# Scores, maxima and their riders in column tiles of 32 on TensorE, with 288 keys for 32 queries

## The chip, the cores and the metric

The kernel runs on one core of one Trainium2 chip. The metric is the device time of one execution in microseconds (us), lower is better. Three executions of the kernel before took 827.12, 827.70 and 828.55 us, median 827.7 us.

## What is computed

A transformer block on 2048 tokens of 512 features: a layer norm, then sliding-window attention and a gated feed-forward network beside each other, joined at the end.

```python
def _A_ref(x, wqkv, wo):            # H = 32 heads, Dh = 16, window W = 256
    scores = einsum("bhqd,bhkd->bhqk", q, k) * Dh ** -0.5
    mask = (idx[:, None] - idx[None, :] >= 0) & (idx[:, None] - idx[None, :] < W)
    p = softmax(where(mask, scores, -1e9)); o = einsum("bhqk,bhkd->bhqd", p, v)
    return o.transpose(...).reshape(B, S, D) @ wo
...
xn = layernorm(x); s = _A_ref(xn, wqkv, wo)
g = silu((silu(xn @ w1) * (xn @ w3)) @ w2)
return x + s * g
```

A query meets itself and the 255 keys before it. That is the fact which the change uses: 64 neighbouring queries together meet 64 + 255 keys, 32 neighbouring queries 32 + 255.

## The kernel before

The tokens are cut into four stretches t of 512, the heads into four groups g of eight, and each group into two pairs p of passes. That makes 32 **units** (t, g, p). Every fp32 product is made of fp16 terms (high and low halves), so a score contracts over 3 x 16 = 48 rows, and two heads lie in the two halves of the partitions (rows 0 and 64).

Attention goes in two passes for each unit.

- **Pass 1** (`pass1`, L605 to L643) finds each query's largest score. `part` makes one of eight score tiles, of 128 queries and two heads: query columns are stationary, and the keys stream past (L623). In all but the first 256 tokens it takes 64 queries at a time and streams the `WIN` = 320 keys that they may meet. With two heads that is four matmuls, each on one quarter of the array (48 rows by 64 columns). Where `narrow` is set, it takes 32 queries at a time, eight matmuls, still with 320 keys. Then VectorE adds the mask MW and takes the maximum along the keys, one instruction for each head (L637). After eight parts the maxima are scaled into NM (L642, L643).
- **`finish`** (L645 to L663) turns the maxima with two matmuls by the identity (L652) into spare columns of a score tile, and sends them by DMA into two more rows of qa, so that pass 2 subtracts them inside its matmul (50 rows).
- **Pass 2** (`pass2`, L678 on) makes the scores the other way round: 64 keys are stationary, and the queries that meet them stream (L699), in pieces of 64 to 320 columns. A chunk fills two banks of PSUM; VectorE masks its edges (L706), ScalarE takes the exponential (L709). `values` multiplies it with V in fp32 on tiles of 64 rows by 32 columns (L727).

**Riders** are small matmuls that use spare columns of a score tile of pass 1: the maxima's turn (L652), sums of squares for the scales of the weights (`powers`, L269 to L273), and the transposes of x for the next stretch (`turn_beside`, L480 to L488), eight fp32 matmuls a rider.

The dense work (the projections L567 and L537, gate and up L900, down L950, output L1001) uses the whole array with 512 moving columns. The order of the work on TensorE is written out by hand: `PLAN` gives each unit five batches of score work. A letter stands for one score tile: W is a chunk of pass 2; M, X and N are parts of pass 1, X into the bank of the value product and N narrow; the last batch, NN, is followed by the values. `spread` puts dense matmuls between batches. VectorE, ScalarE, GpSimd and the DMA queue get their order from a scheduler with priorities, and each of them works in order.

The masks are made once at the start: MW on 64 partitions by VectorE and GpSimd (L198 to L203), then copied to the other 64 with one DMA of SyncE's queue (L1179), between loads of weights (L804).

Of the kernel before, what the change touches and what calls it, by code (L numbers as in the profile page):

```python
# [11 lines left out]
BF16 = mybir.dt.bfloat16  # L12
F16 = mybir.dt.float16
# [8 lines left out]
P = 128  # L22
# [9 lines left out]
TW = S // NT  # L32
KW = TW + 2 * P
WIN = 64 + 2 * P
FB = F // P
NEG = -1e30

# [9 lines left out]
KR = TERMS * DH  # L47
# [32 lines left out]
def tile_block(ctx: ExitStack, tc: tile.TileContext, x, wqkv, wo, w1, w3, w2, out):  # L80
    nc = tc.nc
# [7 lines left out]
    const = pool("const", 1)  # L89
# [88 lines left out]
    def beside_scores(n, f):  # L178
# [4 lines left out]
    identf = const.tile([P, P], F32, name="identf")  # L183
# [11 lines left out]
    nc.gpsimd.affine_select(M1[:, 1, :], M1[:, 1, :], pattern=[[-1, P]], base=0, channel_multiplier=1,  # L195
                            compare_op=ALU.is_ge, fill=NEG)

    MW = const.tile([P, WIN], BF16, name="MW")  # L198
    nc.vector.memset(MW[0:64], 0.0)
    nc.gpsimd.affine_select(MW[0:64], MW[0:64], pattern=[[1, WIN]], base=0, channel_multiplier=-1,  # L200
                            compare_op=ALU.is_gt, fill=NEG)
    nc.gpsimd.affine_select(MW[0:64], MW[0:64], pattern=[[-1, WIN]], base=2 * P, channel_multiplier=1,
                            compare_op=ALU.is_ge, fill=NEG)  # L203


# [5 lines left out]
                                compare_op=ALU.is_gt if k else ALU.is_ge, fill=NEG)  # L211


    NM = [const.tile([P, 64], F16, name=f"NM{i}") for i in range(3)]
    for nm in NM:
        nc.gpsimd.memset(nm, 0.0)

# [40 lines left out]
    def powers(sb, n, p2, inv, s=None):  # L258


        m = sb.shape[-1] // n
        al = small.tile([P, n], F32, name="al")
        if s is None:
            ps = scores_bank()[:, 0, 0:n]
            for i in range(m):
                nc.tensor.matmul(ps, onesb, sb[:, i * n:(i + 1) * n], start=i == 0, stop=i == m - 1)
        else:
            for h in range(2):
                for c in range(2):  # L269
                    for i in range(m):  # L270
                        nc.tensor.matmul(s[64 * c:64 * c + 64, h, WIN:WIN + n],
                                         onesb[64 * h:64 * h + 64, 64 * c:64 * c + 64],
                                         sb[64 * h:64 * h + 64, i * n:(i + 1) * n], start=i == 0, stop=i == m - 1)  # L273

        def rest():
            if s is None:
                nc.vector.tensor_scalar(al, ps, 2.08, 1e-30, op0=ALU.mult, op1=ALU.max)
            else:
                with urgent():
                    nc.vector.tensor_scalar(al, s[:, 0, WIN:WIN + n], 2.08, 1e-30, op0=ALU.mult, op1=ALU.max)  # L280
                    nc.vector.scalar_tensor_tensor(al, s[:, 1, WIN:WIN + n], 2.08, al, op0=ALU.mult, op1=ALU.add)

            nc.vector.tensor_scalar(al.bitcast(I32), al.bitcast(I32), 24, 23, op0=ALU.logical_shift_right,  # L283
                                    op1=ALU.logical_shift_left)
# [114 lines left out]
    def prepare(t):  # L399
# [76 lines left out]
        def turn_beside(b, n, s):  # L476


            if t not in X:
                X[t] = xpool.tile([P, NC, TW], F16, name="XH"), xpool.tile([P, NC, TW], F16, name="XL")  # L480
            xh, xl = X[t]
            for k in range(n, n + 2):
                for h in range(2):
                    for c in range(2):
                        f = k * P + 64 * c
                        rows = slice(64 * h, 64 * h + 64)
                        nc.tensor.matmul(s[64 * c:64 * c + 64, h, WIN + 64 * (k - n):WIN + 64 * (k - n + 1)],
                                         xts[b][rows, f:f + 64], identf[rows, rows], start=True, stop=True)  # L488
            if n:
                give(xts.pop(b))  # L490

            def rest():
                pt = s[:, :, WIN:WIN + P].rearrange("p h (k q) -> p k h q", k=2)
                hi, lo = (a[:, n:n + 2, b * P:(b + 1) * P].rearrange("p k (h q) -> p k h q", h=2) for a in (xh, xl))
                with urgent():
                    nc.vector.tensor_copy(hi, pt)
                    nc.vector.tensor_sub(lo, pt, hi)
                if n:
                    turned[t] = turned.get(t, 0) + 1
            return rest  # L500
# [104 lines left out]
    def pass1(t, g, p):  # L605


        M = small.tile([P, 2, 2, 4], F32, name="M")
        whole = NM[(2 * (t * NG + g) + p) % len(NM)]
        nm = whole[:, 0:32].rearrange("p (b i) -> p b i", b=2)  # L610

        def part(ii, a, beside, narrow):
            qa, ka = QA[t, g], keys(t, g)
            i = t * 4 + ii
            n, mask = ((i + 1) * P, M1.rearrange("p a b -> p (a b)")[:, (1 - i) * P:]) if i < 2 else (WIN, MW)
            s = pso.tile([P, 2, TW], F32, name="po") if beside else scores_bank()

            w = 32 if narrow else 64
            for c in range(0, P, w):
                e = (ii + 3) * P if i < 2 else (ii + 2) * P + 64 * (c // 64 + 1)  # L620
                for r in range(2):
                    rows = slice(64 * r, 64 * r + KR)
                    nc.tensor.matmul(s[c:c + w, r, :n], qa[rows, 2 * p + a, ii * P + c:ii * P + c + w],  # L623
                                     ka[rows, 2 * p + a, e - n:e], start=True, stop=True)
            after = []
            if narrow:
                pass
            elif alone[0] and maxima and (ii, a) != (0, 0):
                after = [f(s) for f in maxima]
                maxima.clear()  # L630
            elif alone[0] and besides:
                after = [besides.pop(0)(s)]
            alone[0] = not after or t * NG + g <= 2
            for r in range(2):
                junk = ppool.tile([P, D], BF16, name="junk", bufs=1)
                with urgent():
                    lasts["maximum"] = nc.vector.tensor_tensor_reduce(  # L637
                        out=junk[:, :n], in0=s[:, r, :n], in1=mask, scale=1.0,
                        scalar=NEG, op0=ALU.add, op1=ALU.max, accum_out=M[:, r, a, ii:ii + 1])
            if (ii, a) == (3, 1):  # L640
                Mf = M.rearrange("p r a i -> p (r a i)")
                nc.vector.tensor_scalar(nm[:, 0, :], Mf, -1.0 / ONE, None, op0=ALU.mult)  # L642
                nc.vector.scalar_tensor_tensor(nm[:, 1, :], Mf, -1.0 / ONE, nm[:, 0, :], op0=ALU.mult, op1=ALU.subtract)  # L643
                maxima.append(finish)
            for f in after:  # L645
                f()

        def finish(s):

            for h in range(2):  # L650
                rows = slice(64 * h, 64 * h + 64)
                nc.tensor.matmul(s[0:64, h, 448:512], whole[rows, 0:64], identh[rows, rows], start=True, stop=True)  # L652

            def rest():
                qa = QA[t, g]
                mt = small.tile([32, P], F16, name="mt")
                with urgent():
                    nc.vector.tensor_copy(mt.rearrange("p (h q) -> p h q", h=2), s[0:32, :, 448:512])
                dm = dpool.tile([32, P], F16, name="dm")
                nc.sync.dma_start(dm, mt)  # L660
                for r in range(2):
                    nc.sync.dma_start(qa[64 * r + KR:64 * r + KR + 2, 2 * p:2 * p + 2, :].rearrange("p a q -> p (a q)"),
                                      dm.rearrange("(b r i) q -> r b (i q)", b=2, r=2)[r])  # L663
            return rest
        return [lambda *kind, ii=ii, a=a: part(ii, a, *kind) for ii in range(4) for a in range(2)]
# [12 lines left out]
    def pass2(t, g, p):  # L678
# [14 lines left out]
        def scores(c):  # L693
            qa, ka = QA[t, g], keys(t, g)
            s = scores_bank()
            for o, h, a, (m, k, n, _, _) in pieces(c):
                for r in range(2):
                    rows = slice(64 * r, 64 * r + KR + 2)
                    nc.tensor.matmul(s[64 * h:64 * h + 64, r, o:o + 64 * n], ka[rows, 2 * p + a, 64 * (m + 4):64 * (m + 5)],  # L699
                                     qa[rows, 2 * p + a, 64 * (m + k):64 * (m + k + n)], start=True, stop=True)  # L700
            which, *_, masks = chunks[c]
            sv = s.rearrange("p r (a k q) -> p (r a) k q", a=len(which), q=64)
            for first, by, n, kind, of in masks:
# [472 lines left out]
    qk[0][0]()  # L1176
    qk[1][0]()
    wv[0]()
    nc.sync.dma_start(MW[64:P], MW[0:64])  # L1179
    for i, k in enumerate((0, 2, 1)):  # L1180
        nc.sync.dma_start(MK[64:P, i], MK[0:64, k])
    load(0, 0)
# [152 lines left out]
```

## Time and profile before

| | |
|---|---|
| time, median of 3 | 827.7 us (827.12 to 828.55) |
| span of the profiled execution | 824.7 us |
| between the span and the median | 3.0 us |
| TensorE matmul busy | 803.9 us, 97% |
| TensorE weight loads | 380.7 us (beside the matmuls) |
| VectorE | 632.2 us, 77% |
| ScalarE | 388.8 us, 47% |
| GpSimd | 205.6 us, 25% |

The profiled execution's own time is known as its span, from the first to the last instruction; the 3.0 us around it lie outside the trace. In the rows that follow, PE is TensorE's matmuls, PEld its weight loads, DVE is VectorE, ACT ScalarE, POOL GpSimd and SPq the DMA queue of SyncE. A row of the timeline gives start and duration in us, engine, line, operation, tile written and tiles read, and their shapes; "48\*64 48x320" is a matmul with 48 rows by 64 columns of weights and 320 moving columns. Matmuls overlap: the duration of one is its whole way through the array, so the pace is read from starts, not from durations.

### The profile page before, as it was taken

How to read it: one execution, taken by the hardware profiler on the slowest of the kernel's cores; microseconds unless marked ns; L12 is line 12 of the kernel's file. 1: busy time of each engine (PE TensorE's matmuls, PEld its weight loads, DVE VectorE, ACT ScalarE, POOL GpSimd, SP SyncE). 2: the span in 40 equal slices, each digit the busy share in tenths (PEclk: the TensorE clock that was granted, in tenths of full speed). 3: DMA queues.
4: the chain of work that ended last, by engine and by line, in shares of the span. 5: the costliest groups of instructions: out<-in, count | busy, mean ns of one | idle time of the engine just before them, and what ended most of it. 6: DMA issues, size and time to landing. Idle time of an engine off the chain costs nothing. (4 is left out here: it accounts for less than half of the span.)

```text
span 824.7 us, 22891 instructions
## 1 busy us (share of the span) xinstructions
PE 803.9 (97%) x8924; PEld 380.7 (46%) x8924; DVE 632.2 (77%) x2021; ACT 388.8 (47%) x562; POOL 205.6 (25%) x355
## 2 busy tenths in 40 slices
PE   8999989999999999999999999999999999999998
PEld 4434435444445444444444444444444444444444
DVE  8788878887798678879878887778777787676435
ACT  6889775634435434344343444442433344343511
POOL 2238174332223203121211111230201113030201
PEclk9999989999999999999999999999999999999999
DMA  9978566266543354544433344434434353343101
GB/s 283 267 230 237 194 177 191 73 170 186 160 122 84 98 154 124 161 117 135 134 105 100 108 109 138 132 119 113 142 85 144 91 131 102 101 132 91 56 21 53
DMA packets 95325, 110.66 MB, mean 134 GB/s; under 512 B 17200, under 2 KB 60528, under 8 KB 95216
## 3 DMA queue, kind: packets, MB, share of 16 engines
q1 hardware_dynamic: 94928, 108.67, 45.9%
q8 instruction: 70, 1.15, 0.6%
q10 hardware_dynamic: 288, 0.52, 0.2%
q14 instruction: 39, 0.32, 0.1%
HBM read 76.28 MB, written 28.57 MB: 127 GB/s over the span
## 5 line engine op out<-in xcount | busy, mean ns | idle before, releaser
L311 POOL TENSOR_TENSOR slot<-slot,slot 128x256 f16<-128x256 f32 (+1 forms) x228 | 151.1, 690 | 522.3 <-ACT slot L929 406.9
L900 PE MATMUL m<-XH,slot 128*128 128x512 f16 x896 | 269.0, 382 | 6.3 <-DVE slot L924 3.2
L709 ACT ACTIVATE pt<-s,es 128x1024 f32<-128x1024 f32 x152 | 167.7, 1113 | 198.3 <-DVE s L706 196.4
L900 PEld LDWEIGHTS <-slot 128*128 128x128 f16 x1344 | 125.4, 98 | 162.6 <-issue 18.9
L900 PE MATMUL m<-XL,slot 128*128 128x512 f16 x448 | 170.5, 381 | 0.0
L950 PE MATMUL m<-slot,slot 128*128 128x512 f16 x672 | 156.5, 380 | 1.5 <-DVE slot L580 0.7
L706 DVE TENSOR_TENSOR s<-s,MK 128x256 f32<-128x256 f32 (+2 forms) x280 | 118.3, 435 | 49.4 <-PE s L699 47.0
L637 DVE CUSTOM_DVE_ANT_0 junk<-s,MW 128x320 bf16<-128x320 f32 x276 | 134.1, 486 | 24.6 <-PE s L623 15.8
L950 PEld LDWEIGHTS <-slot 128*128 128x128 f16 x672 | 61.9, 98 | 79.7 <-issue 9.0
L637 DVE CUSTOM_DVE_ANT_0 junk<-po,MW 128x320 bf16<-128x320 f32 x172 | 83.6, 486 | 5.4 <-DVE al L283 0.5
L727 PE MATMUL po<-pt,V 64*32 64x320 f32 (+4 forms) x2880 | 77.2, 342 | 0.1
L929 ACT CAST slot<-slot 128x512 f16<-128x512 f32 x56 | 34.5, 616 | 76.0 <-DVE slot L924 71.8
L915 ACT ACTIVATE slot<-m,sgs 128x512 f32<-128x512 f32 x56 | 38.3, 684 | 54.9 <-PE m L900 54.8
L727 PEld LDWEIGHTS po<-pt,V 64*32 64x32 f32 x2880 | 51.1, 106 | 21.6 <-issue 0.8
L919 DVE SCALAR_TENSOR_TENSOR slot<-slot,m 128x512 f32<-128x512 f32 x56 | 38.3, 684 | 27.6 <-ACT slot L915 27.3
L699 PE MATMUL s<-qa,KA 50*64 50x320 f16 (+3 forms) x1472 | 58.3, 260 | 0.6 <-ACT pt L709 0.6
L699 PEld LDWEIGHTS <-KA 50*64 50x64 f16 x1472 | 30.3, 106 | 55.3 <-issue 32.7
L623 PE MATMUL s<-KA,qa 48*64 48x320 f16 (+3 forms) x824 | 45.5, 295 | 4.3 <-ACT pt L709 3.2
L924 DVE SCALAR_TENSOR_TENSOR slot<-m,slot 128x512 f32<-128x512 f32 x56 | 38.5, 687 | 10.6 <-PE m L900 10.0
L974 DVE SCALAR_TENSOR_TENSOR slot<-m,dsc,slot 128x512 f32<-128x512 f32 x48 | 35.9, 747 | 13.2 <-PE m L950 13.0
L567 PE MATMUL m<-XH,whi 128*128 128x512 f16 x120 | 44.7, 381 | 0.0
L567 PE MATMUL m<-XL,whi 128*128 128x512 f16 x120 | 44.5, 379 | 0.0
(162 smaller groups left out, 870.6 us busy)
## 6 DMA issues: line engine op xcount, KB each, us to landing
slot<-dW SPq DMA_DIRECT2D x126, 256.0 KB
slot<-in_B_w_dram SPq DMA_DIRECT2D x42, 256.0 KB
dW<-slot SPq DMA_DIRECT2D x42, 256.0 KB
slot<-in_A_x_dram SPq DMA_DIRECT2D x30, 256.0 KB
KA<-dK SPq DMA_DIRECT2D x24, 288.0 KB
qa<-dQ SPq DMA_DIRECT2D x32, 192.0 KB
dQ<-slot SPq DMA_DIRECT2D x16, 256.0 KB
dK<-slot SPq DMA_DIRECT2D x16, 256.0 KB
```

Source lines behind the costliest of these rows:

```text
L311: op(out[:, c], a[:, c], b[:, c])
L567: nc.tensor.matmul(cell["pp"], a[:, k, c, :], b[:, c, :], start=(c, i) == parts[0][0], stop=(c, i) == parts[-1][-1])
L623: nc.tensor.matmul(s[c:c + w, r, :n], qa[rows, 2 * p + a, ii * P + c:ii * P + c + w], ka[rows, 2 * p + a, e - n:e], start=True, stop=True)
L637: lasts["maximum"] = nc.vector.tensor_tensor_reduce(out=junk[:, :n], in0=s[:, r, :n], in1=mask, scale=1.0, scalar=NEG, op0=ALU.add, op1=AL ...
L699: nc.tensor.matmul(s[64 * h:64 * h + 64, r, o:o + 64 * n], ka[rows, 2 * p + a, 64 * (m + 4):64 * (m + 5)], qa[rows, 2 * p + a, 64 * (m + k ...
L706: nc.vector.tensor_add(v, v, MK[:, kind, of:of + n, :].unsqueeze(1).to_broadcast([P, 2 * len(which), n, 64]))
L709: nc.scalar.activation(pt, s, AF.Exp, scale=es)
L727: nc.tensor.matmul(cell["po"][32 * i:32 * i + 32, h, 64 * (m + k):64 * (m + k + n)], V[64 * h:64 * h + 64, (4 * t + m // 2) % VB, hd * VW: ...
L900: nc.tensor.matmul(cell[k], w[:, (a * NC + c) * P:(a * NC + c + 1) * P], b[:, c, :], start=c == 0 and i == 0, stop=c == NC - 1 and i == 2)
L915: nc.scalar.activation(sg, cell[0], AF.Tanh, scale=sg_scale[:, f:f + 1])
L924: lasts["emptied"] = nc.vector.scalar_tensor_tensor(sg, cell[1], 0.5 * HS / (WS * XS)**2, sg, op0=ALU.mult, op1=ALU.mult)
L950: nc.tensor.matmul(ps, hh[:, a * TW + b * P:a * TW + (b + 1) * P], w[:, c * D:(c + 1) * D], start=f == f0 and i == 0, stop=f == f1 - 1 and ...
```

## The change

All matmuls of the score tiles take 32 columns of the array. Pass 1 always takes 32 queries at a time, with 288 keys (`MWIN`) in place of 320, and its mask and VectorE's instruction shrink with it. In pass 2 each stationary set of 64 keys becomes two of 32, with the same moving columns. The riders are split in the same way. MW is made on 32 partitions and copied with three DMAs in place of one. NM shrinks from 64 columns to 32.

```diff
+MWIN = 32 + 2 * P
...
-    MW = const.tile([P, WIN], BF16, name="MW")
-    nc.vector.memset(MW[0:64], 0.0)
+    MW = const.tile([P, MWIN], BF16, name="MW")
+    nc.vector.memset(MW[0:32], 0.0)
...
-    NM = [const.tile([P, 64], F16, name=f"NM{i}") for i in range(3)]
+    NM = [const.tile([P, 32], F16, name=f"NM{i}") for i in range(3)]
...
-                for c in range(2):
+                for c in range(0, P, 32):
                     for i in range(m):
-                        nc.tensor.matmul(s[64 * c:64 * c + 64, h, WIN:WIN + n],
-                                         onesb[64 * h:64 * h + 64, 64 * c:64 * c + 64],
+                        nc.tensor.matmul(s[c:c + 32, h, WIN:WIN + n], onesb[64 * h:64 * h + 64, c:c + 32],
                                          sb[64 * h:64 * h + 64, i * n:(i + 1) * n], start=i == 0, stop=i == m - 1)
...
-                    for c in range(2):
-                        f = k * P + 64 * c
+                    for c in range(0, P, 32):
+                        f = k * P + c
                         rows = slice(64 * h, 64 * h + 64)
-                        nc.tensor.matmul(s[64 * c:64 * c + 64, h, WIN + 64 * (k - n):WIN + 64 * (k - n + 1)],
-                                         xts[b][rows, f:f + 64], identf[rows, rows], start=True, stop=True)
+                        nc.tensor.matmul(s[c:c + 32, h, WIN + 64 * (k - n):WIN + 64 * (k - n + 1)],
+                                         xts[b][rows, f:f + 32], identf[rows, rows], start=True, stop=True)
...
-            n, mask = ((i + 1) * P, M1.rearrange("p a b -> p (a b)")[:, (1 - i) * P:]) if i < 2 else (WIN, MW)
+            n, mask = ((i + 1) * P, M1.rearrange("p a b -> p (a b)")[:, (1 - i) * P:]) if i < 2 else (MWIN, MW)
...
-            w = 32 if narrow else 64
+            w = 32
             for c in range(0, P, w):
-                e = (ii + 3) * P if i < 2 else (ii + 2) * P + 64 * (c // 64 + 1)
+                e = (ii + 3) * P if i < 2 else (ii + 2) * P + c + w
...
-                nc.tensor.matmul(s[0:64, h, 448:512], whole[rows, 0:64], identh[rows, rows], start=True, stop=True)
+                nc.tensor.matmul(s[0:32, h, 448:512], whole[rows], identh[rows, rows], start=True, stop=True)
...
             for o, h, a, (m, k, n, _, _) in pieces(c):
-                for r in range(2):
-                    rows = slice(64 * r, 64 * r + KR + 2)
-                    nc.tensor.matmul(s[64 * h:64 * h + 64, r, o:o + 64 * n], ka[rows, 2 * p + a, 64 * (m + 4):64 * (m + 5)],
-                                     qa[rows, 2 * p + a, 64 * (m + k):64 * (m + k + n)], start=True, stop=True)
+                for j in range(0, 64, 32):
+                    for r in range(2):
+                        rows = slice(64 * r, 64 * r + KR + 2)
+                        at = 64 * (m + 4) + j
+                        nc.tensor.matmul(s[64 * h + j:64 * h + j + 32, r, o:o + 64 * n], ka[rows, 2 * p + a, at:at + 32],
+                                         qa[rows, 2 * p + a, 64 * (m + k):64 * (m + k + n)], start=True, stop=True)
...
-    nc.sync.dma_start(MW[64:P], MW[0:64])
+    for i in range(1, 4):
+        nc.sync.dma_start(MW[32 * i:32 * i + 32], MW[0:32])
```

More of the change, by code (lines that the diff above doesn't have):

```diff
@@ L196, in tile_block @@
                             compare_op=ALU.is_ge, fill=NEG)
-    MW = const.tile([P, WIN], BF16, name="MW")
-    nc.vector.memset(MW[0:64], 0.0)
-    nc.gpsimd.affine_select(MW[0:64], MW[0:64], pattern=[[1, WIN]], base=0, channel_multiplier=-1,
+    MW = const.tile([P, MWIN], BF16, name="MW")
+    nc.vector.memset(MW[0:32], 0.0)
+    nc.gpsimd.affine_select(MW[0:32], MW[0:32], pattern=[[1, MWIN]], base=0, channel_multiplier=-1,
                             compare_op=ALU.is_gt, fill=NEG)
-    nc.gpsimd.affine_select(MW[0:64], MW[0:64], pattern=[[-1, WIN]], base=2 * P, channel_multiplier=1,
+    nc.gpsimd.affine_select(MW[0:32], MW[0:32], pattern=[[-1, MWIN]], base=2 * P, channel_multiplier=1,
                             compare_op=ALU.is_ge, fill=NEG)
@@ L609, in pass1 @@
         whole = NM[(2 * (t * NG + g) + p) % len(NM)]
-        nm = whole[:, 0:32].rearrange("p (b i) -> p b i", b=2)
+        nm = whole.rearrange("p (b i) -> p b i", b=2)
         def part(ii, a, beside, narrow):
```

## The prediction

> **What bounds the kernel now.** I read the page first, then the busy time by stage, then who waited for whom on TensorE.
>
> ```profile
> span 824.7 us, 22891 instructions
> ...
> PE 803.9 (97%) x8924; PEld 380.7 (46%) x8924; DVE 632.2 (77%) x2021; ACT 388.8 (47%) x562; POOL 205.6 (25%) x355
> ```
>
> The span is 824.7 us; the median of the runs is 827.7 us, so 3.0 us lie around it. I work in differences and subtract them from the median. Matmuls fill 97% of the span. In the table by stage the second column is the length, the third PE's busy time:
>
> ```profile
> 0.00:60.00 60.00, 54.38 (x330) 24.59 (x331) 48.32 (x183) 47.72 (x99) 18.75 (x53) 1.00 0.93 263
> 60.00:130.00 70.00, 64.93 (x655) 30.23 (x653) 56.69 (x211) 58.02 (x111) 36.17 (x63) 0.95 0.68 206
> 130.00:240.00 110.00, 106.73 (x1226) 51.52 (x1228) 89.81 (x318) 51.11 (x73) 36.85 (x64) 1.00 0.49 145
> 240.00:730.00 490.00, 487.46 (x5897) 231.52 (x5890) 386.30 (x1202) 203.57 (x246) 96.61 (x150) 1.00 0.43 119
> 730.00:824.70 94.70, 90.39 (x828) 42.80 (x826) 51.05 (x112) 28.36 (x35) 17.17 (x26) 1.00 0.22 63
> ```
>
> From 240 to 730 us PE idles 2.5 of 490 us: there only a shorter stream of matmuls shortens the kernel, and a longer one lengthens it by as much. The other idle time lies mostly in the first 240 us (5.6, 5.1 and 3.3 us), where VectorE ends it:
>
> ```profile
> PE m L900 <- DVE slot L924: 3.2, 1, 3.2
> PE s L623 <- ACT pt L709: 3.2, 3, 1.3
> PE m L900 <- DVE slot L580: 1.6, 2, 1.4
> PE m L900 <- DVE slot L919: 1.4, 3, 0.7
> ```
>
> **The pace of the stream.** One batch in the timeline, with the dense work on both sides:
>
> ```profile
> 735.28 0.59 PE L900 MATMUL m<-XH,slot 128*128 128x512 f16 x2
> ...
> 735.93 0.59 PE L900 MATMUL m<-XH,slot 128*128 128x512 f16 x2
> 736.36 0.38 PE L900 MATMUL m<-XL,slot 128*128 128x512 f16 x1
> 736.67 0.41 PE L699 MATMUL s<-qa,KA 50*64 50x320 f16 x8
> 736.91 0.31 PE L623 MATMUL s<-KA,qa 48*64 48x320 f16 x4
> 737.05 0.30 PE L623 MATMUL po<-KA,qa 48*64 48x320 f16 x4
> 737.29 2.76 PE L1001 MATMUL m<-slot,slot 128*128 128x512 f16 x12
> ```
>
> Three dense matmuls advance the stream from 735.28 to 735.93: 0.217 us each, 0.423 ns a column. Four score matmuls of 320 columns on four quarters of the array advance it from 736.91 to 737.05, 0.14 us: 320 columns at the same pace, so the four run abreast. Into the batch goes 736.67 - 736.36 - 0.22 = 0.09 us, and out of it 0.24 - 0.14 = 0.10 us: a change of the tile shape costs nearly 0.1 us. The question is whether eight matmuls of 32 columns go as fast as four of 64. The last batch of a unit has them already:
>
> ```profile
> 747.28 0.47 PE L623 MATMUL s<-KA,qa 48*32 48x320 f16 x16
> 747.56 2.53 PE L727 MATMUL po<-pt,V 64*32 64x256 f32 x96
> ```
>
> Sixteen narrow matmuls, two score tiles, take 0.28 us, again 0.14 each. So a set costs its moving columns, not its number of matmuls, at this size.
>
> **The change, part by part.**
>
> *Shorter maxima on TensorE.* VectorE's rows count the tiles:
>
> ```profile
> L637 DVE CUSTOM_DVE_ANT_0 junk<-s,MW 128x320 bf16<-128x320 f32 x276 | 134.1, 486 | 24.6 <-PE s L623 15.8 <-PE s L487 2.4
> L637 DVE CUSTOM_DVE_ANT_0 junk<-po,MW 128x320 bf16<-128x320 f32 x172 | 83.6, 486 | 5.4 <-DVE al L283 0.5 <-DVE mt L658 0.3
> L637 DVE CUSTOM_DVE_ANT_0 junk<-po,M 128x256 bf16<-128x256 f32 x16 | 6.8, 423 | 0.4
> ```
>
> 276 + 172 = 448 maxima of 320 keys, two to a tile: 224 tiles. Each loses 32 columns: 32 x 0.423 = 13.5 ns, **-3.0 us**, all on PE's stream, which is the path.
>
> *No change of tile shape inside a batch.* In the first stretch (`FIRST_PLAN`) the last batch is one wide part and then the values, 64 columns and then 32:
>
> ```profile
> 202.63 0.33 PE L623 MATMUL s<-KA,qa 48*64 48x320 f16 x4
> 202.89 2.05 PE L727 MATMUL po<-pt,V 64*32 64x320 f32 x72
> ```
>
> Four matmuls take 0.26 us here against 0.14: about 0.1 us goes into the change of shape. The part or its rider stands like this in eight units: 8 x 0.09 = **-0.7 us**.
>
> *Small pieces and riders.* The number of matmuls doubles in pass 2 (1472 to 2944), in the riders' transposes (192 to 384) and sums (72 to 144), and rises in pass 1 from 1200 to 2048. Their columns per tile stay. Where pieces are 64 or 128 columns long, the feeding of matmuls could become the limit:
>
> ```profile
> 401.21 0.64 PE L699 MATMUL s<-qa,KA 50*64 50x320 f16 x24
> 401.68 0.31 PE L623 MATMUL po<-KA,qa 48*64 48x320 f16 x4
> ...
> 423.99 0.40 PE L487 MATMUL po<-identf,slot 64*64 64x64 f32 x16
> 424.33 0.39 PE L537 MATMUL m<-wvh,XH 128*128 128x512 f16 x1
> ```
>
> Two chunks with small pieces, 24 matmuls, take 0.47 us; each quarter gets 512 columns a chunk, 1024 x 0.423 = 0.43 us, so they go at the columns' pace too. After the change 48 must start in this time, 9 ns each. A rider of transposes, 16 records (eight fp32 matmuls in two goes), takes 424.33 - 423.99 - 0.10 = 0.24 us; 32 records need 7.5 ns each. How fast can they come? The tail of the values has the smallest pieces on 32 columns; number of matmuls in brackets:
>
> ```profile
> 725.52:725.98 0.46, 0.46 (x40) 0.43 (x24) 1.00 0.56 214
> 725.52:725.68 0.16, 0.16 (x24) 0.15 (x9) 1.00 0.00 0
> ```
>
> 24 in 0.16 us is 6.7 ns each, 40 in 0.46 us is 11.5 ns each. These bound it. Since a rider or chunk stands behind dense work, in which matmuls can be queued, I take a value near the first: 8.2 ns. The chunks then cost nothing, the 24 riders 32 x 8.2 - 240 = 22 ns or some more each: **+0.7 us**. At 6.7 ns it is nothing. At 11.5 ns a rider costs 32 x 11.5 - 240 = 128 ns, 24 of them 3.1 us; the 48 chunks with 24 matmuls (two in each of the 24 units behind the first stretch) 24 x 11.5 - 217 = 59 ns, 2.8 us; the first stretch's 32 chunks of 20 matmuls 13 ns, 0.4 us: +6.3 us.
>
> *Entry and exit of a batch.* At the start the first weights have to be loaded. The batch above spends 0.24 us on 320 + 192 columns, 0.217 us at the pace, so 23 ns go there; the narrow one 0.28 us on 640 columns, 0.271 us, so 9 ns: 14 ns less with 32 columns. At the end the last of eight matmuls starts later than the last of four, by at most 4 x 6.7 = 27 ns. I set them against each other: 0, between -14 and +13 ns in each of some 130 batches (four in each of 32 units), 1.8 us either way.
>
> *VectorE.* From 320 to 256 keys the instruction goes from 486 to 423 ns, 1.0 ns a key; 32 keys are 32 ns, 448 times: 14 us less on an engine that isn't the bound. Its cover is PE, busy 97%. It shows only where PE waits for VectorE. Of such waits the four rows above hold 6.2 us from VectorE; a stall is shortened by what VectorE's queue gained since it last stood idle, some 4 to 8 maxima, 0.13 to 0.26 us. I take 0.1 us for each of the six waits on VectorE in those rows: **-0.6 us**, between 0 and all 6.2 us. The scheduler also swaps neighbours on ScalarE and VectorE in the first 130 us (in the changed order a sum of squares, L858, stands ahead of the weight split L305); each such swap moves a 0.6 to 0.7 us instruction past one, so 1 us either way.
>
> *SyncE's queue.* Two more copies of MW stand ahead of the weight loads:
>
> ```profile
> 7.78 0.56 SPq L1179 DMA_DIRECT2D MW<-MW  x1
> 8.66 1.94 SPq L1181 DMA_DIRECT2D MK<-MK  x3
> 10.84 1.74 SPq L804 DMA_DIRECT2D slot<-in_B_w_dram  x3
> ```
>
> That is 2 x 0.56 = 1.1 us later for each load behind them. The DMA engines are 93% busy in the first 60 us (the table by stage), so the loads wait for bandwidth more than for their issue, and I count 0; without that cover 1.1 us.
>
> **Sum.** -3.0 - 0.7 + 0.7 - 0.6 = -3.6 us: 827.7 - 3.6 = 824.1, **824.1 us** (span 821.1).
>
> **Rivals.**
>
> *Slower: feeding becomes the limit.* Small matmuls come every 11.5 ns when they don't lie ready, as in the tail of the values. Then +6.3 us stands in the place of +0.7: 824.1 + 5.6 = 829.7 us. It decides where a matmul takes longer than about 10 ns: at 10.7 ns riders and chunks lose 24 x 102 + 48 x 40 ns = 4.4 us, about as much as the rest brings (3.0 + 0.7 + 0.6). For it: nothing in the trace shows 48 weight loads and 48 matmuls in 0.43 us. Against it: 24 starts in 0.16 us.
>
> *Much slower: every start has a floor.* The 96 records of the values take 2.46 us from 747.56 (the dense work follows at 750.02), 25.6 ns each. If that were a floor for each matmul and not the pace of their columns, pass 2's 2944 and pass 1's 2048 would take 4992 x 25.6 = 128 us; now they take 1472 x 0.47 / 24 = 29 us and 256 tiles x 0.14 = 36 us. That is +63 us, 887 us with the rest. Against it: the sixteen narrow ones above start within 0.28 us, 17.5 ns each, and the tail of the values is faster yet. The Trainium skill, "TensorE: Matmul & The Clock Gate", section "Wait — 56ns, not 53.3ns?", states such a floor: starts never come closer than about 25 ns, however small the matmul. This trace does not bear it out for tiles that run abreast.
>
> *Same: the stream's gain turns into waits.* PE arrives earlier at banks that VectorE or ScalarE still hold, and the two copies of MW cost their 1.1 us. For it: the 3.2 us of PE waiting for L709's exponentials, which the change doesn't shorten. Against it: VectorE, ahead of ScalarE in that chain, gains five times what PE does, 14 against 3 us. About 827.2 us.
>
> *Faster still: the throttle's dip goes.* The wait of 3.2 us in front of L924 is followed by a half clock:
>
> ```profile
> 110.70:114.20 3.50, 0.29 (x2) 0.01 (x1) 3.33 (x9) 1.83 (x4) 1.61 (x3) 0.84 0.67 190
> 114.20:119.90 5.70, 5.66 (x31) 2.06 (x31) 3.77 (x13) 5.67 (x12) 5.61 (x9) 0.50 0.74 249
> ```
>
> The clock column reads 0.50 for 5.7 us, a loss of 2.9 us. If the wait becomes short enough, it is saved: 824.1 - 2.9 = 821.2 us. The order on VectorE there is unchanged, which speaks for the dip's staying. A new wait of this kind would cost the same.
>
> **Chances.** Forecast (822 to 826): 0.54. Dip gone: 0.12. Same: 0.15. Feeding, or a new stall of its size in the first 130 us: 0.17. Floor: 0.02. The range leaves out the floor and the ends of the waits; it takes in the dip (with 1.8 us for entry and exit, down to 819.5) and the feeding: 819.5 to 830. A measurement tells some 0.2%, 1.7 us, from no change. Faster: 0.54 + 0.12 = 0.66. Within: 0.15 and 0.02 of a mild feeding, 0.17. Slower: 0.15 + 0.02 = 0.17.
>
> **What would show it.** Right: maxima tiles 0.13 us apart in the timeline with eight matmuls each; VectorE's maxima near 454 ns; the batch of two small chunks still 0.47 us; PE's busy time 800 us or a little less. Wrong: 48 matmuls of two chunks over 0.5 us, or riders over 0.3 us (feeding); more than 15 us of waits on VectorE or ScalarE for PE (same); a half clock elsewhere.

## The result, and the profile after

The changed kernel takes 837.6 us (median of 6 runs, 833.1 to 842.0) against 827.6 us before: 1.2% slower, ratio 1.0124 with the interval 1.0102 to 1.0146. The forecast was 824.1 us, its range ended at 830. The profiled run is the quickest of the six, 833.1 us with a span of 831.3 us and a mean granted clock of 0.999; the other five ran at 0.986 to 1.000. So the profile shows 6.6 us of the loss in the span, and the other runs lose up to 9 us more that it does not show. The clock alone doesn't order them: the run at 1.000 took 837.8 us. Each of the six runs is 1.8 us longer than its span. Of the 3.0 us that were put around the span before, some 1.2 are therefore no time outside the trace: the profiled execution was faster than the median. A forecast made of differences does not feel that.

First the head of the page, then the table by stage (length, then busy time of PE, PE's weight loads, VectorE, ScalarE, GpSimd, then clock, DMA share and GB/s):

```profile
span 831.3 us, 28441 instructions
...
PE 802.5 (97%) x11700; PEld 384.0 (46%) x11700; DVE 615.5 (74%) x2021; ACT 387.5 (47%) x562; POOL 204.7 (25%) x355
```

```profile
0.00:60.00 60.00, 53.87 (x416) 24.52 (x417) 47.18 (x180) 47.12 (x98) 17.64 (x51) 1.00 0.93 261
60.00:130.00 70.00, 60.56 (x828) 28.40 (x827) 53.03 (x198) 55.38 (x108) 37.10 (x64) 1.00 0.64 198
130.00:240.00 110.00, 104.68 (x1751) 52.17 (x1748) 88.08 (x319) 52.63 (x75) 36.97 (x64) 1.00 0.48 142
240.00:730.00 490.00, 486.56 (x7584) 232.51 (x7583) 370.52 (x1201) 201.98 (x245) 91.84 (x145) 1.00 0.42 120
```

PE's busy time fell by 1.4 us, yet the span grew by 6.6: PE's idle time grew by 8.0, from 20.8 us to 28.8. The stream of matmuls did not get shorter, though. Before, PE's busy time held a half clock at 114 to 120 us, a loss of 2.9 us, which is missing here. From 60 to 130 us PE idles 9.4 us (5.1 before), from 130 to 240 us 5.3 (3.3), from 240 to 730 us 3.4 (2.5). Who PE waits for (total, times, longest):

```profile
PE s L623 <- ACT pt L711: 6.3, 5, 2.1
PE m L902 <- DVE slot L926: 3.3, 1, 3.3
PE m L537 <- DVE slot L580: 2.1, 3, 1.6
PE s L623 <- DMA qa<-dQ: 1.6, 2, 1.3
```

L711 is the exponential that was L709 (3.2 us before), L926 the product that was L924 (3.2 us). So the wait in front of the missing half clock is as long as it was.

Two places show how the new waits arise. ScalarE at 93 to 99 us, first changed, then before (start, length, engine, line, operation; in brackets the idle time before it and what ended it):

```profile
96.48 0.63 ACT L860 ACTIVATE sqa<-slot 128x512 bf16<-128x512 f32 x1 [3.00 <-DMA slot<-in_B_w_dram]
...
97.11 1.10 ACT L711 ACTIVATE pt<-s,es 128x1024 f32<-128x1024 f32 x1
98.11 0.68 ACT L917 ACTIVATE slot<-m,sgs 128x512 f32<-128x512 f32 x1
```

```profile
92.85 1.11 ACT L709 ACTIVATE pt<-s,es 128x1024 f32<-128x1024 f32 x1 [0.97 <-DVE s L706]
93.86 0.68 ACT L915 ACTIVATE slot<-m,sgs 128x512 f32<-128x512 f32 x1
95.80 0.63 ACT L858 ACTIVATE sqa<-slot 128x512 bf16<-128x512 f32 x1 [1.26 <-DMA slot<-in_B_w_dram]
```

Before, the exponential and the gate go first and the sum of squares waits for its weights behind them. Now the square stands ahead; ScalarE idles 3.0 us for the DMA with the exponential queued behind, and PE stands 1.31 us:

```profile
98.26 0.30 PE L623 MATMUL s<-KA,qa 48*32 48x256 f16 x8 [1.31 <-ACT pt L711]
```

VectorE at 222 us of the changed kernel, and at 214 us of the kernel before:

```profile
221.73 0.35 DVE L770 RECIPROCAL dr<-dr 128x32 f32<-128x32 f32 x1 [3.32 <-DMA dr<-dd]
222.00 0.63 DVE L580 SCALAR_TENSOR_TENSOR slot<-m,slot 128x512 f16<-128x512 f32 x1
```

```profile
213.99 0.69 DVE L580 SCALAR_TENSOR_TENSOR slot<-m,slot 128x512 f16<-128x512 f32 x1 [0.15 <-ACT slot L576]
218.11 0.35 DVE L768 RECIPROCAL dr<-dr 128x32 f32<-128x32 f32 x1 [3.43 <-DMA dr<-dd]
```

The reciprocal waits for its DMA in both. Before, the product L580 that empties PE's bank is ahead of it; now it is behind, and PE stands 1.65 us:

```profile
222.68 0.38 PE L537 MATMUL m<-wvh,XH 128*128 128x512 f16 x1 [1.65 <-DVE slot L580]
```

Neither instruction is touched by the diff. The scheduler chose their places.

### The profile page after: what moved, and what is told of

It is laid out like the page before. It is cut to its first block, busy times and chain, and to the rows that moved or that the text cites. A ratio compares the mean times of both kernels' runs of the same rounds, so it can differ in the third digit from the quotient of the medians.

```text
span 831.3 us, 28441 instructions
## 1 busy us (share of the span) xinstructions
PE 802.5 (97%) x11700; PEld 384.0 (46%) x11700; DVE 615.5 (74%) x2021; ACT 387.5 (47%) x562; POOL 204.7 (25%) x355
## 4 chain that ended last, share of the span: by engine, by line
PE 68%; DVE 9%; ACT 8%; DMA 6%; issue 3%; SPq 3%; POOL 2%; ACTq 0%; DVEq 0%; POOLq 0%
PE m L902 23%; PE m L952 15%; PE po L729 7%; PE m L567 6%; PE s L701 4%; PE m L1003 4%; PE m L537 3%; DVE junk L637 2%; PE s L623 2%; ACT pt L711 2%; POOL slot L311 2%; DVE s L708 2%; DMA slot<-in_B_w_dram 2%; ACT slot L314 2%; SPq L777 1%
## 5 line engine op out<-in xcount | busy, mean ns | idle before, releaser
L711 ACT ACTIVATE pt<-s,es 128x1024 f32<-128x1024 f32 x152 | 167.1, 1113 | 216.2 <-DVE s L708 211.8
L637 DVE CUSTOM_DVE_ANT_0 junk<-s,MW 128x288 bf16<-128x288 f32 x276 | 124.9, 453 | 22.8 <-PE s L623 13.6
L637 DVE CUSTOM_DVE_ANT_0 junk<-po,MW 128x288 bf16<-128x288 f32 x172 | 77.8, 452 | 4.9
L701 PE MATMUL s<-qa,KA 50*32 50x320 f16 (+4 forms) x2944 | 59.2, 255 | 0.8 <-ACT pt L711 0.5
L701 PEld LDWEIGHTS <-KA 50*32 50x32 f16 x2944 | 30.5, 89 | 54.9 <-issue 30.1
L623 PE MATMUL s<-KA,qa 48*32 48x288 f16 (+2 forms) x1296 | 45.0, 279 | 8.8 <-ACT pt L711 6.3
L926 DVE SCALAR_TENSOR_TENSOR slot<-m,slot 128x512 f32<-128x512 f32 x56 | 38.4, 686 | 9.1 <-PE m L902 8.8
L623 PEld LDWEIGHTS <-qa 48*32 48x32 f16 x2048 | 31.6, 91 | 28.6 <-issue 22.1
```

The source lines that it names most:

```text
L637: lasts["maximum"] = nc.vector.tensor_tensor_reduce(out=junk[:, :n], in0=s[:, r, :n], in1=mask, scale=1.0, scalar=NEG, op0=ALU.add, op1=AL ...
L701: nc.tensor.matmul(s[64 * h + j:64 * h + j + 32, r, o:o + 64 * n], ka[rows, 2 * p + a, at:at + 32], qa[rows, 2 * p + a, 64 * (m + k):64 * ...
L711: nc.scalar.activation(pt, s, AF.Exp, scale=es)
L926: lasts["emptied"] = nc.vector.scalar_tensor_tensor(sg, cell[1], 0.5 * HS / (WS * XS)**2, sg, op0=ALU.mult, op1=ALU.mult)
```

## The experiments

Theories: QUEUE, the two further copies of MW delay the loads behind them on SyncE; FEED, TensorE can't take in so many small matmuls; ORDER, the scheduler, which orders all engines but TensorE, reorders them for the finer matmuls and so makes the waits. Each time stands beside the runs of the kernel before on the same chip.

### The copies of MW, and the tiles alone

`e1_one_copy` makes MW on 64 partitions and copies it once; `e2_old_three_copies` is the kernel before with its copy cut in three.

```diff
 e2
-    nc.sync.dma_start(MW[64:P], MW[0:64])
+    for c in (slice(0, 32), slice(32, 48), slice(48, 64)):
+        nc.sync.dma_start(MW[64 + c.start:64 + c.stop], MW[c])
```

> The changed kernel, but MW is made on 64 partitions (two 32-row halves, two more selects on GpSimd) and copied with one DMA, as before. Theory QUEUE (three copies of MW hold SyncE's queue for 2.2 us in place of 0.56, every load behind them is late, and the waits of the first 240 us come from that): the first wait for qa is back near 0.5 us, the waits of TensorE before 240 us fall by 4 to 6 us, time 831 to 833 us. Theory ORDER (the scheduler's swaps on VectorE and ScalarE make the waits): no change, 836 to 839 us. Theory FEED (small matmuls come no faster than every 10.5 ns) explains only 4 us of stream, about as much as the shorter maxima save, and expects no change here.

> The kernel before, with its one copy of MW split into three DMAs of 32, 16 and 16 partitions; nothing else is changed. QUEUE: SyncE's queue stands 1.2 to 1.7 us longer at the copies, qa comes over 1 us later, time 830 to 834 us. ORDER: as before, 827.6 us, unless the scheduler moves other instructions too. FEED: 827.6 us.

Measured: 836.9 us (ratio 1.0112, 1.0088 to 1.0136) and 828.4 us (1.0014, 1.0000 to 1.0028). One copy leaves the loss; three cost the old kernel 1.2 us, 2.3 at most. QUEUE falls as the cause of the 10 us. The copies do have a price: PE's waits for qa come to 0.5 us before and 0.6 in `e1_one_copy`, with one copy, and to 1.6 in `e2_old_three_copies` as in the changed kernel, with three (one later kernel with three copies, `e7_old_order_act`, has 0.5). The second kernel also has ScalarE's order changed in 48 of 515 places: not every other order costs.

`e3_tiles_only` splits all score tiles and riders to 32 columns but keeps 320 keys, MW and its copy.

> All score tiles and riders on 32 columns, but still 320 keys in the maxima, and MW made and copied as before: the split of the tiles alone. FEED: the riders' transposes go from 0.24 to 0.34 us and batches with two small chunks lose 0.05 us, +4 us, less 0.7 for the changes of shape and 0.4 at the riders of the maxima: 830 to 831 us. QUEUE: 827.6 us, with the wait for qa as before. ORDER: 833 us or more if the scheduler's swaps come from the split, with the waits before 240 us as in the changed kernel.

Measured: 837.8 us (1.0133, 1.0109 to 1.0157), with ScalarE's order different from before in 118 places and from the changed kernel in 37. The tile split alone brings the time and, nearly, the order.

### The order, forced

VectorE, ScalarE and GpSimd have the same instructions, one by one, in both kernels (SyncE two copies more); only their sequence differs, in 105 of 515 places on ScalarE, 204 of 1499 on VectorE, 30 of 360 on GpSimd and 180 of 821 on SyncE. So one kernel can be given the other's sequence, by edges that set the order of issue and wait for nothing:

```diff
+    for e, (n, packed) in _ORDER.items():
+        l = made[e]
...
+        at = struct.unpack(f"<{n}H", zlib.decompress(base64.b85decode(packed)))
+        for a, b in zip(at, at[1:]):
+            tc.add_manual_dep(l[b], l[a].name, mybir.DependencyInfo(mybir.DependencyClass.NoSync, mybir.DependencyReason.DATA),
+                              reason="order")
```

Four kernels, in this order: `e5_old_order`, `e6_new_order`, `e7_old_order_act`, `e11_old_order_act_dve`; e5 and so on for short.

> The changed kernel, all of it, with one thing more: ScalarE, VectorE, GpSimd and SyncE issue their instructions in exactly the order of the kernel before (SyncE's two further copies of MW stand right behind the first). TensorE's matmuls are those of the changed kernel. ORDER (the order that the scheduler chose on ScalarE and VectorE puts sums of squares that wait for a DMA ahead of exponentials, and this makes the waits of the first 240 us): 826 to 829.5 us; the waits of TensorE at the scores' line on ScalarE's pt, 6.3 us in the changed kernel, go back to about 3 us, and what is left against the kernel before is the queue's 1.2 us at most and a stream that is equal. MATMULS (the narrow matmuls themselves bring the time: their feeding and the pace at which they free the banks, whatever the other engines' order): 835 to 839 us.

> The mirror image: the kernel before, its matmuls and its 320 keys untouched, with ScalarE, VectorE, GpSimd and SyncE in the order of the changed kernel (without the two copies of MW that it does not have). ORDER: 834 to 838 us, with TensorE's waits at the scores' line on pt at 5 to 6 us and ScalarE's squares waiting for DMA for about 10 us. MATMULS: 826 to 829 us.

> The changed kernel with ScalarE alone in the order of the kernel before; the other engines are ordered by the scheduler again around that (VectorE stays as in the changed kernel in nearly every place, 202 of its 1499 instructions stand elsewhere than before). ORDER, if ScalarE's order is what counts: 827 to 831 us, near the kernel with all four engines in the old order. ORDER, if VectorE's or SyncE's order counts as much: 832 to 837 us. MATMULS: 835 to 839 us.

> The changed kernel with ScalarE and VectorE in the order of the kernel before, SyncE and GpSimd free. All four in the old order gave 828.1 us, ScalarE alone 830.6. VECTORE (the rest is VectorE's order): 827 to 829 us. SYNCE (the rest is the order of loads and stores on SyncE): 829.5 to 832 us.

Measured, with the ratio to the kernel before:

| kernel | us | ratio (95%) |
|---|---|---|
| changed, all four in the old order (e5) | 828.1 | 1.0012 (0.9999 to 1.0025) |
| before, all four in the new order (e6) | 837.0 | 1.0124 (1.0100 to 1.0148) |
| changed, ScalarE in the old order (e7) | 830.6 | 1.0057 (1.0026 to 1.0088) |
| changed, ScalarE and VectorE (e11) | 828.0 | 0.9991 (0.9978 to 1.0004) |

This decides it from both sides: the kernel before, with not one matmul changed, is as slow as the changed kernel once it has the new order, and the changed kernel with the old order is as fast as before, within its interval. By the medians ScalarE's order carries some 7 us and VectorE's 2.5; by the ratios it is 5.5 and 5.5, since two of e7's six runs lie well above the rest (830.3 to 837.4 us). SyncE and GpSimd, left free in e11, cost nothing that shows. In e6 PE waits at the same places:

```profile
PE s L623 <- ACT pt L709: 5.9, 5, 2.3
PE m L537 <- DVE slot L580: 3.6, 1, 3.6
```

and with the old order in the changed kernel (e5) these lines read

```profile
PE s L623 <- ACT pt L711: 4.0, 3, 2.0
...
PE m L537 <- DVE slot L580: 0.3, 1, 0.3
```

Waits are not the whole of it. The profiled execution of e6 has a span of 837.0 us, 12.3 more than before. PE idles 25.8 us of it (20.8 before) and is busy 811.2 us (803.9), with not one matmul changed. The further busy time is the clock, which before was 0.95 and 1.00 in these two stretches:

```profile
60.00:130.00 70.00, 62.91 (x591) 28.54 (x589) 52.79 (x194) 54.33 (x104) 35.82 (x63) 0.93 0.63 196
130.00:240.00 110.00, 103.23 (x1191) 49.50 (x1190) 83.73 (x302) 50.60 (x73) 35.43 (x62) 0.95 0.46 140
```

That is 0.07 x 70 + 0.05 x 110 = 10.4 us of clock, against 3.5 before. The clock is 0.50 at 98, 118, 173 and 224 us, for 3 to 7 us each time, behind or within waits of 1.6, 3.0, 2.3 and 3.6 us. A wait does not always bring it: the changed kernel's profile has the wait of 3.3 us at 115 us and no half clock there. So part of the price of a new order is half clock, and that part changes from run to run.

### Which instructions

Two runs in each direction cut ScalarE's order in two: the 48 sums of squares (L236, L860; before L235, L858), and all the rest. Of the squares 14 stand elsewhere in the changed order, most of them one or two places earlier and four of them ten to twelve. The kernels are `e9_squares_back`, `e10_squares_early`, `e13_rest_back` and `e14_rest_new`, in this order.

> The changed kernel, in which ScalarE keeps its changed order for all but the 48 sums of squares (L236 and L860); these stand behind as many other instructions as in the kernel before. The other engines are free. SQUARES (of the new order it is the squares, issued up to twelve places earlier, that delay exponentials and gates): 829 to 832 us, as with all of ScalarE in the old order (830.6). OTHER (swaps among the exponentials, the splits L314 and L315 and the copies L931 bring it): 834 to 838 us.

> The mirror image: the kernel before, in which only the 48 squares on ScalarE stand where the changed kernel has them; all else on ScalarE in the old order, the other engines free (VectorE has 40 instructions elsewhere, SyncE 3). SQUARES: 831 to 836 us, with TensorE's waits at the scores' line on pt at 5 us or more. OTHER: 826 to 829 us.

> The changed kernel, in which all of ScalarE but the squares stands in the old order; the 48 squares keep the early places of the changed kernel. REST (the exponentials behind splits and copies carry it): 830 to 832 us, as with all of ScalarE put back (830.6). EITHER (either part alone makes late what the other part would have made late too, so that putting one back brings little): 834 to 837 us. SUM (the parts add, with the squares at the 3.1 us that they cost in the kernel before): 833 to 834.5 us.

> The kernel before, in which all of ScalarE but the squares stands in the changed order, the squares in their old places; the other engines are free. REST: 833 to 836 us. EITHER: also above the kernel before, 830 to 834 us. If ScalarE's order without the squares costs nothing by itself: 826.5 to 828.5 us.

Measured: in the changed kernel 837.1 us with the squares put back (1.0113, 1.0089 to 1.0137) and 838.8 with the rest put back (1.0126, 1.0105 to 1.0147), against 830.6 with both. In the kernel before 830.8 with the squares early (1.0036, 1.0023 to 1.0048) and 828.8 with the rest moved (1.0022, 1.0010 to 1.0034). SQUARES and REST both fail as the one cause: in the changed kernel either half alone brings the loss back. That is what EITHER says, but its numbers missed: it expected 834 to 837 us for e13 (838.8) and 830 to 834 for e14 (828.8). In the old kernel the squares cost some 3 us and the rest 1 to 2, so the two do not add up to 7 there. That squares alone do harm is shown by the old kernel: there, too, the early square makes the exponential wait,

```profile
95.30 0.63 ACT L858 ACTIVATE sqa<-slot 128x512 bf16<-128x512 f32 x1 [3.52 <-DMA slot<-in_B_w_dram]
...
95.93 1.09 ACT L709 ACTIVATE pt<-s,es 128x1024 f32<-128x1024 f32 x1
```

Why the halves do not add stays open; the other engines were free in these four and were ordered anew around each.

On VectorE six of the sixteen reciprocals had moved ahead of one or two instructions. These alone, all else held, in `e16_reciprocals_early` and `e17_reciprocals_back`:

> The kernel before, with all engines held in their own order but for six of the sixteen reciprocals of the softmax's sums (L768), which wait for a DMA: on VectorE they go ahead of one or two instructions, as in the changed kernel (at 218 us ahead of the product L580). RECIPROCAL (one such swap makes TensorE wait at 216 us and one at 703 us): 2 to 4.5 us above the kernel before, 829.3 to 832 us, of it 1.8 us or more at 216 us and 1.0 us at 703 us. If PE's lag at those places has another cause: 826.5 to 828.5 us.

> The mirror image: the changed kernel, held in its own order but for the same six reciprocals, which go back behind these one or two instructions. RECIPROCAL: 2 to 4.5 us under the changed kernel (837.6), 833 to 835.6 us, and the wait at the bank of L537 at 216 us is gone. Otherwise 836.5 to 838.5 us.

Measured: 830.6 us (1.0040, 1.0026 to 1.0055) and 836.0 us (1.0097, 1.0076 to 1.0117). Six small swaps cost the old kernel 3.2 us. The one at 219 us does what it did in the changed kernel:

```profile
219.07 0.35 DVE L768 RECIPROCAL dr<-dr 128x32 f32<-128x32 f32 x1 [3.57 <-DMA dr<-dd]
219.34 0.63 DVE L580 SCALAR_TENSOR_TENSOR slot<-m,slot 128x512 f16<-128x512 f32 x1
```

and PE stands for it:

```profile
220.03 0.38 PE L537 MATMUL m<-wvh,XH 128*128 128x512 f16 x1 [2.05 <-DVE slot L580]
```

Put back, that wait is gone, but the whole gains 1.6 us, less than expected, and its interval overlaps that of the changed kernel. The loss expected near 703 us has another cause: the changed kernel's wait there, 0.72 us at 708.53, stays in e17 and does not come in e16.

### Feeding

`e4_split_rider` cuts the riders' transposes of the kernel before into two of 32 moving columns each, on tiles of 64. `e8_cut_pieces` takes e5 and cuts every piece of 320 columns into 128 and 192: more matmuls, the same columns.

```diff
 e8
-                        nc.tensor.matmul(s[64 * h + j:64 * h + j + 32, r, o:o + 64 * n], ka[rows, 2 * p + a, at:at + 32],
-                                         qa[rows, 2 * p + a, 64 * (m + k):64 * (m + k + n)], start=True, stop=True)
+                        for u, v in ((0, 2), (2, 5)) if n == 5 else ((0, n),):
+                            nc.tensor.matmul(s[64 * h + j:64 * h + j + 32, r, o + 64 * u:o + 64 * v], ka[rows, 2 * p + a, at:at + 32],
+                                             qa[rows, 2 * p + a, 64 * (m + k + u):64 * (m + k + v)], start=True, stop=True)
```

> The kernel before on tiles of 64 columns, with each transpose of the riders cut along its moving columns, 2 x 32 in place of 64: 32 records a rider in place of 16, the same columns. FEED: a rider takes 32 x 10.6 = 0.34 us in place of 0.24, whatever the width of its tiles. If only the columns counted, it would stay at 0.24 to 0.26 us. Time within 3 us of 827.6 either way.

> The changed kernel with the four engines in the old order (the first kernel of this call), and in pass 2 each piece of 320 columns is cut into one of 128 and one of 192: a chunk of small pieces has 32 matmuls instead of 24, one of two pieces 24 instead of 16, with the same columns. FEEDING (about 10.3 ns for each small matmul): two small chunks and a part behind them, 0.86 us in the changed kernel, take 0.16 us more, the 32 chunks of the first stretch some 0.07 us each; in all 5 to 8 us above the first kernel of this call. COLUMNS (a chunk costs its 512 columns on each tile): no more than 1 us above it.

Measured: e4 834.3 us in its one run, 7 us above before. A rider of 32 records takes 0.29 us more: 429.07 - 428.44 - 0.10 = 0.53 us, 16.7 ns a record.

```profile
428.44 0.69 PE L489 MATMUL po<-identf,slot 64*64 64x32 f32 x32
429.07 0.39 PE L539 MATMUL m<-wvh,XH 128*128 128x512 f16 x1
```

24 riders make the 7 us, and ScalarE's order is as before in this kernel, so it isn't a matter of order. But 0.53 us is above what either theory gave; each record also loads 64 columns of fp32 weights, so the run does not separate feeding from loading, and I count it as a miss. e8 took 835.4 us in one run, 7.3 above the median of e5, whose ten runs lie between 825.4 and 829.7; FEEDING expected 5 to 8. Two small chunks and a part, in e5 and then in e8:

```profile
400.76 0.68 PE L701 MATMUL s<-qa,KA 50*32 50x320 f16 x48
401.23 0.36 PE L623 MATMUL po<-KA,qa 48*32 48x288 f16 x8
401.53 0.82 PE L952 MATMUL m<-slot,slot 128*128 128x512 f16 x3
```

```profile
407.33 0.84 PE L702 MATMUL s<-qa,KA 50*32 50x128 f16 x64
407.95 0.38 PE L623 MATMUL po<-KA,qa 48*32 48x288 f16 x8
408.26 0.82 PE L953 MATMUL m<-slot,slot 128*128 128x512 f16 x3
```

From the first start to the dense work: 0.77 us with 56 matmuls, 0.93 with 72. Sixteen more with no more columns cost 0.16 us, 10 ns each.

### A version ahead of both

`e12_two_moves`: the shorter maxima, one copy of MW, the old order, and two instructions moved forward by hand. `e15_before_two_moves`: the same two moves in the kernel before.

> A version that could beat both: the changed kernel with MW in one copy, ScalarE, VectorE and SyncE in the old order, and two instructions moved forward by hand. On ScalarE the exponential for which TensorE waits 2.0 us at 93 us goes ahead of the square that waits for its DMA and of two more; its scores are masked at 90.0 us and it starts at 91.84, so up to 1.8 us. On VectorE the product L926 for which TensorE waits 3.2 us at 115 us goes from 114.36 to behind the reduction at 111.98, so some 2.2 us. LOCAL (each wait is that instruction's place and nothing else is late behind it): 823 to 825.5 us. CHAIN (the next late thing takes the gain): 826 to 828.5 us.

> The kernel before with its own order and the same two instructions moved forward as in the version that measured 826.1 us: the exponential of 92 us ahead of three squares, the product L924 of 114 us to behind the reduction. Here TensorE waits 1.20 us for the one and 3.25 us for the other. If the version's lead is the moves' own: 825 to 826.5 us, as fast as with the change or faster. If it needs the shorter maxima: 827 to 828.5 us.

Measured: 826.1 us (0.9980, 0.9970 to 0.9991) and 827.8 us (0.9995, 0.9984 to 1.0007). The moves do nothing that shows by themselves in the kernel before, and in the changed one the next late instruction takes their gain: in e12 the wait of 3.2 us at 115 us is 1.0 us at 112, but PE then stands 1.3 us at 115 us for VectorE's maxima and 1.9 us at 117 us for an exponential (CHAIN). The change, one copy, the old order and the moves together are ahead by 1.5 us: the only kernel here whose interval lies below the kernel before. It overlaps the interval of e11, which has neither the one copy nor the moves, and that of e15, so a lead over these isn't shown. Which of the parts it needs beside the change wasn't tried. One hint is that PE's waits for qa come to 0.6 us in it, and to 1.9 and 2.3 in e5 and e11 with their three copies.

## Why the prediction was wrong, step by step

*Shorter maxima: right.* Two tiles follow each other in 0.13 us, eight matmuls each, and VectorE's instruction takes 453 ns:

```profile
738.50 0.41 PE L701 MATMUL s<-qa,KA 50*32 50x320 f16 x16
738.73 0.31 PE L623 MATMUL s<-KA,qa 48*32 48x288 f16 x8
...
738.86 0.31 PE L623 MATMUL po<-KA,qa 48*32 48x288 f16 x8
739.11 0.61 PE L902 MATMUL m<-XH,slot 128*128 128x512 f16 x2
```

```profile
L637 DVE CUSTOM_DVE_ANT_0 junk<-s,MW 128x288 bf16<-128x288 f32 x276 | 124.9, 453 | 22.8 <-PE s L623 13.6 <-PE s L487 2.8 <-PE m L537 0.2
```

*Entry and exit of a batch, 0: right.* In the same rows the chunk takes 0.23 us to the first part, 0.24 before, and the last part 0.25 us to the dense work with 32 columns fewer, 0.24 before. One sets off the other, as the prediction had it.

*No change of shape inside a batch: right.* From the part to the values it was 0.26 us and is 0.13:

```profile
207.47 0.32 PE L623 MATMUL s<-KA,qa 48*32 48x288 f16 x8
207.60 2.03 PE L729 MATMUL po<-pt,V 64*32 64x320 f32 x72
```

*Small pieces and riders, +0.7 us: too small by some 3.6 us.* A part and a rider of transposes took 0.50 us to the dense work (423.83 to 424.33) and take 0.61; two small chunks and a part took 0.71 (401.21 to 401.92) and take 0.77, though the part is 0.013 shorter. Before, and then in the changed kernel:

```profile
401.92 0.82 PE L950 MATMUL m<-slot,slot 128*128 128x512 f16 x3
...
423.83 0.33 PE L623 MATMUL po<-KA,qa 48*64 48x320 f16 x4
```

```profile
429.50 0.32 PE L623 MATMUL po<-KA,qa 48*32 48x288 f16 x8
429.63 0.54 PE L487 MATMUL po<-identf,slot 64*32 64x64 f32 x32
430.11 0.39 PE L537 MATMUL m<-wvh,XH 128*128 128x512 f16 x1
```

```profile
406.83 0.68 PE L701 MATMUL s<-qa,KA 50*32 50x320 f16 x48
407.30 0.36 PE L623 MATMUL po<-KA,qa 48*32 48x288 f16 x8
407.60 0.82 PE L952 MATMUL m<-slot,slot 128*128 128x512 f16 x3
```

24 x (0.11 + 0.07) = 4.3 us. The value of 8.2 ns a matmul was the mistake. Of the two signs of feeding one failed: the 48 matmuls still take 0.47 us up to the part's first start, and the delay shows only behind the part. The other came true: a rider takes 430.11 - 429.63 - 0.10 = 0.38 us, over 0.3. The rival of feeding reckoned with 10.7 ns; the runs give about 10. With 4.3 for 0.7 and nothing from VectorE the sum would have been 827.7 - 3.0 - 0.7 + 4.3 = 828.3 us, and the changed kernel in the old order takes 828.1 (its interval reaches from 827.1 to 829.3), so a match to 0.2 us is partly luck. Between the same two batches of values, twenty units apart, PE is busy 449.7 us before (271.50 to 723.70), 449.9 in the changed kernel (276.97 to 730.17) and 449.1 in e5 (271.13 to 722.08), all at full clock. So the tiles themselves win nothing and lose nothing that shows.

*Floor of 25 ns: refuted.* 48 matmuls in 0.47 us are 9.8 ns each. The Trainium skill, "TensorE: Matmul & The Clock Gate", section "Wait — 56ns, not 53.3ns?", has starts never closer than about 25 ns; here, on eight tiles abreast, they are.

*VectorE, -0.6 us of waits: not seen.* Its busy time fell by 16.7 us, more than the 14 of the sum. The wait on L926 is 3.3 us, as it was; in e5, with the order unchanged, PE idles 8.6 us from 60 to 240 us (6.4 + 2.2) against 8.3 before:

```profile
60.00:130.00 70.00, 63.63 (x932) 30.11 (x930) 54.97 (x208) 57.47 (x110) 36.52 (x64) 0.98 0.66 205
130.00:240.00 110.00, 107.81 (x1760) 53.47 (x1762) 89.56 (x322) 51.86 (x74) 36.83 (x64) 1.00 0.49 149
```

*The scheduler's swaps, "1 us either way": the step that failed.* I had seen squares stand ahead of splits, and priced a swap by the length of the instruction that moves, 0.6 to 0.7 us. Its price comes from the time that the moved instruction waits: 3.0 us for a square whose weights are still on their way, 3.3 us for a reciprocal. Of these PE stood 1.3 and 1.65 us at the two places shown. And I looked at the first 130 us only and for swaps of neighbours; squares had moved by up to twelve places, and the reciprocal swap sits at 218 us. In all it is 9 to 10 us (837.6 against 828.1 in the changed kernel, 837.0 against 827.2 in the kernel before), waits and half clock together. Which instructions carry it is shown for six reciprocals (3.2 us in the old kernel) and, with the other engines free, for the squares (some 3 us there); how the rest comes about stays open. The nearest rival, a new stall of feeding's size in the first 130 us, had this kind of loss at half its size.

*SyncE's queue, 0 with a bound of 1.1 us: the bound was nearer.* The three copies cost the old kernel 1.2 us (0 to 2.3), and PE's waits for qa grow from 0.5 to 1.6 us there and in the changed kernel. The cover, DMA engines busy to 93%, did not hold.

*Throttle's dip, a rival:* the dip is gone from this profile, but not because the wait became short, as the rival had it. Its 2.9 us are why PE's busy time is lower here, and the new waits took more. Nor does the dip belong to the wait: in `e2_old_three_copies` the wait is 3.2 us too, and the mean clock is 1.000.

## What to carry to other kernels

Where a scheduler orders the engines, a diff changes more than its lines: compare the issue order of every engine, and for each instruction that moved forward ask what it waits for, not how long it runs. An instruction that waits for a DMA blocks all that stands behind it on its engine (here 3.0 us on ScalarE at 96 us, 3.3 us on VectorE at 222 us). To tell a change from its order, give each kernel the other's order; here both directions gave the same answer.

## What the runs showed of the hardware

Small matmuls on eight tiles abreast, each with its own weight load, come at about 10 ns each when their columns don't fill the time (16 more cost 0.16 us in e8), and 32 records of fp32 transposes on tiles of 64 columns at 16.7 ns each (e4). Kernels in which TensorE stands more often ran at a lower mean clock: 0.988 to 0.994 in e6 and 0.986 to 1.000 in the changed kernel, against 0.994 to 0.998 in e5 and 0.993 to 1.000 in the kernel before. An estimate from the means over the runs (0.992, 0.994, 0.996 and 0.997): some 4 of e6's 9.8 us and 2 to 3 of the changed kernel's 9.5 are clock, if each us at half clock costs half a us. By this estimate the waits are the larger part.
